# A sparse-attention and gated-MLP kernel: every convolution tap on VectorE, and a new order and new engine choices for all its jobs

## The chip, the cores and the metric

The kernel runs on one core of one Trainium2 chip. The metric is the time of one execution on the device in microseconds (us). Three runs of the kernel before gave 330.38, 330.82 and 330.89 us; the median, 330.82 us, is the time before.

## The reference

Three stages follow one another (B = 2, H = 8, S = 768, D = 64; the model width is 512). Attention sees 16 keys to either side and 24 summaries of 32 keys each; a gated layer mixes the rows with a 768 x 768 matrix; a second gated layer has a convolution of three taps along the rows.

```python
def attention(q, k, v):
    k_sum = k.reshape(B, H, 24, 32, D).max(axis=3)
    v_sum = v.reshape(B, H, 24, 32, D).mean(axis=3)
    scores = concat([where(abs(i - j) < 16, q @ k.T / sqrt(D), -1e9),
                     q @ k_sum.T / sqrt(D) + log(32)])
    a = softmax(scores)
    return a @ concat([v, v_sum])

def first_layer(x):
    u, v = split(maximum(x @ w_in, 0))
    v_n = (v - mean(v)) / sqrt(var(v) + 1e-6)
    return (u * (w_spatial @ v_n + b_spatial)) @ w_out

def second_layer(x):
    h = maximum(x @ w_in2, 0)                       # 512 -> 1024
    conv = sum(conv_w[k] * shift(h, k - 1) for k in range(3))
    return (h * sigmoid(conv)) @ w_out2             # 1024 -> 512
```

## The kernel before

All products are made at fp32 accuracy from three fp32r matmuls (`mm3`, L320 to L322: high times high, high times low, low times high). So every operand is split into a high part (a cast, L295, on ACT or POOL) and a low part (a subtraction, L289, on DVE or POOL).

**Attention** runs in 16 groups G0 to G15. A group is four head-rows of one batch; two groups share one pair of loads (n = group // 2). Each group goes through scores (PE, L472, L479, L485, into one of two PSUM tiles `s`), row maximum (DVE, L489), exponentials (ACT, L493, 12 pairs of instructions), total and reciprocal (DVE, L496, L499), the normalising multiplication (L502, POOL or DVE), two transposes (PE, L506, into the single PSUM tile `pt`) each followed by a copy out (L528, ACT or DVE), the product with the values (PE, L512) and the split of its result (L533, L534). The values of a pair of groups come by the DMA of L386 into `vwin`; there are two such buffers, used in turn, so the values of G4 (n = 2) can be loaded only when the L512 products of G0 (n = 0) are done. PE makes the block means of the values (L428), DVE and POOL the block maxima of the keys (L408, L414).

**First layer.** The weights are rounded by hand into fp32r parts (L304 to L311, the two long ones L309 and L311 on DVE). Products u and v (L550), the statistics of v, the spatial product with its operands split 768 columns wide (L600 to L602, the subtraction is L289), the gate. `w_out` is merged with the second layer's `w_in2` (L664, L665), and the merged matrix is rounded again (L689 to L699).

**Second layer.** `i2(f)` for f = 0 to 7 makes one eighth of h; `conv_gate(f)` (L736 to L790) makes its convolution: tap k = 1 is a scaling on ACT (L748), tap k = 0 a multiply-add on DVE (L752). The tap k = 2 is a second L752, except for f in `TAPDMA` = (0, 2): there ACT scales h into a tile of its own (L748, `tmp`), and two DMAs, issued on POOL's queue, add this tile to the sum (L765, one for each batch). Sigmoid (ACT, L772), gate (L775, L789). The last product uses a scheme of blocks with seven products instead of eight, with sums of blocks before (L716; some by a DMA on POOL's queue, `TDMA`, L714) and after (L874), and stores the output (L870).

**What sets the order.** `Plan.add` (L105) lists jobs, each with the engines that may run it and with what it reads and writes. `Plan.order` (L127) issues them in the order of a table `ORDER` (two letters name one job), and `PICK` says, for a job that more than one engine may run, which one. Every engine then runs its instructions in exactly that order. Where the plan sees PE idle early on, it puts warm-up matmuls with no result there (L932).

```python
if f in TAPDMA:
    add(scaled(zp, hp, 2, n), r + 0.6, [hp.tok(), tok("conv")], [zp.tok()], lock=True)
add({"DVE": (us, lambda bs=bs: tap(0, bs))}, r + 1, [hp.tok(), tok("conv")], [cp.tok()], lock=True)
if f in TAPDMA:
    for b in range(b0, b1):
        def join(b=b):
            POOL.dma_start(two(ct)[:, b, :S - 1], two(z)[:, b, 1:], accum_op=ADD)
        dma_add(r + 2, S, join, [z.tok(b * S, (b + 1) * S)], [ct.tok(b * S, (b + 1) * S)])
else:
    add({"DVE": (us, lambda bs=bs: tap(2, bs))}, r + 2, [hp.tok(), tok("conv")], [cp.tok()], lock=True)
```

Of the kernel before, what the change touches and what calls it, by code (L numbers as in the profile page):

```python
# [50 lines left out]
ORDER = (
    "ABASACAFAEAUAGAiATADAHAjAgAkAAAhALAqAVAWAIAMBKBYAXArAYA3BaAZAsANAJBbBZBLA4BcAbAtBEAKBiAuBFAaBMAOA5B8AlCRBNBjA6A7AvBGAcBO"
    "BkCTAwA8AmAxCUB9BlAyAPBHBmBvCSCDB+AnBPDJCVApBnAzA9B-AoA+CbBwBxBRA-DKA0CcCdBABoBpCoC5A1DIBIByDLCEA2BBBdBzCpBqBQBCCeDHBDB0"
    "CFAdDRBeBrBTCGCqB1CHDSAQCrBJC6CfBfCWCsC1BgB2ARC7BhDeCgB3BsDTB4ETEeDfBtBuCXEgBSChCYB5CiC2CZCjDUB6CkCBDVCACtFOEUEhB7DrEfC8"
    "CuEnCCC9BUClDWDgEoDwCaCvDhCwCmCxEpDiDjE0FPCnDXCyCzFMDMDYDxDZDsE1FBC0DaDkFCDNBVDODPCICJDlEqFVC4C+E2DbF8DmDcDnDtDyDdDQCKC-"
    "DoErFWFNEsDpAeFiEtDqBWE3AfF9C3EuE4FXFjDuDvDzEvD1D2D3F6D4CLDAD0D6CMEwFkBXD5E5EiD7DBE6FYEVCNCODCFvCPDDEXFZDEFlE7D8EjCQD9D+"
    "D-E8EYEEEkGmFFDFDGEFEAEGJ5EmE9ElEZEWF7EaEHEBEbFzECFGFDEcFHGDGQExFIFJFaEIEdFmE+EDGlEOGdFQEPGREyEJFKEKF1F0E-FLEQEzGkGSELGn"
    "EREMFAESHRGEF2F3FRGeFbENFxF4HHFcGFGTGfGgF5HIFdGhGiFSHSFwGGFnGjG6FTF+G7GtHJGUHTFeFoHKFpHUFqFfGHHLFrFUGuFgFsHVHbFhGIGvFtFu"
    "J6GwHMHlHmHcHNHdG8HnGJHOHeGKIyGVIiHfGLGMF-GAG9HoGWFEHvHWHwGXHgGBGCGYHxHpHqH5GZGaGbGNIDH6FyGoIEGxGcGyGOGPG+GzHyHXG-GpG0Gq"
    "H7HYHPGsLNItHrH8HzHhHQHiH9G1G2H+IFIIGrHAINIOHBHjHCH0HsG3HDH1HkHEIuG4H2G5IJLPHZIKHtHFIdHuH-H3IPHGILIAIaISITIeIzIvIfIjIMIG"  # L60
    "IBIbIHIgIhIUI9HaIVICJHH4InLOJIJJIkJlIoIcJ7IWI0JbIQIRIXI3IYIpI+IZI-I4JAJcI6JRIlJmImIwI5IqJKI7JSLbLQIxJdJBLUI1JTI2JnJUKHLR"
    "JLJvJCJDI8JoIrJEJeIsJVJpJwJ9JMJWJFJqJfJxKRKIJgJrLWJyJNKlJGK5KvKwKbJzLDK6LSJsKJJXLEJ0KSJOKcLTJhJiJ1JtLVKmJ+K7KKJ2LFKTLXJ3"
    "KdLYJYJ-KxJPLiLGLZJZKnLdLaKUKVJuKAKyJaLcLeJ8LfLgJQLhLkKLK8KMLpLjKoKzJ4KBLlJjLmKeKWKCKNJkKfLrK9KOKXLwLnLHMrKgKDLoLqKYLsLt"
    "LyKZKpKELIMhKqMiKhKrM1LuK+LvKFLxKsKaLzKtL0NJKPMsKGNKMjL3L1KQK0K-K1L+LJL2M2MtL5M-KuL4M3L6M4K2NLL7KiNAMAL8NdL9NMLKMkNBNnKj"
    "L-MFLAMuNCMBNTMlLBKkNDMCMvNUNoMDMHMmNVMnK3NpMELCMGK4MIMMM5NqNeNEMJMwMOOpMTMKMoMLLLNFMNMxOqM6M7MyNWNNMPMpMQO7LMNXMVMRO8MS"
    "MaNGMqM8MUMzMWNrNHOvNYOwMXNxNONsM9O9MYM+MZNtNfO1NPMbNZOrNQOxOyOzNyMcN4MdPTMeOsO+NzNuNgMfN0PBOtO2N-NhO3PHN1OuO0MgNRN6NaNi"
    "M0N5PIPJN7PKOAO4OBN8PCPUO5N9PVO-PZPDOGO6NIOIPjPEPAS9NvP0OHOUNbPaONPWNjPeOJNwPNPfNkPLPbNcOKOCNlODNSN2NmPOPcOLPkPFPgPlPXOE"
    "PmPhPPOPN3OVOWPYOOP1S+OiPMTDPdOXPnPiOYOQOZPQOMPGORP+TEPoP5ObP6OFPqP-PpP2OjOdOcPrOkP7PsP8P3OeQAOfOSPRPtQBPuOlQQQRP9OgP4QS"
    "N+PSQCQDQmQTOTPvOaOmQUPwOhQwQrQEQVQLQMQWOnQFQXTFQNQOS-QYQnQxQoQsQGQHOoQtQuPxQyQpPyQzTAQPQ9RHQZQaRCTJRDQITGTPQJQbRIRETBRF"
    "PzTLQcQKQdTCQvTHRJRKTKQ+TMTNRSQ-RAQfTITOQ0QqRcTRQeRdTWRXTVRTQ1URTQReTZQhTSUlRUTcQ2QgRGQ3QiRVQjRLTTRfTURYRZUSTdRBRaRMRnUT"  # L70
    "Q4RoRsRpRtQ5QkTgRNRqRWROQlRgRPRQQ6RuRbRvRRSASFRhQ7RrUgSBUWRiRjSCSGUmSDRxSHRwR2Q8RlUhR3RkUnUUSKSoUpUoR4S1R8UbUqUXStRmR+UY"
    "SIUiRyUZSJRzR0SESZSeUVSuSPSvUaSLUcSMUwU7SNSaSbSQUxSfR1S2UjUrSpU8R5UdUySRSwSqSOSgScSSUeSjR6SVS3SkR7ShSdVZVdSTUkU0SrSiTaSx"
    "T3UfTeSUVaR9SlSmVeSXSWSnUzU1ThVbTxSzVfU2SyT9ULR-UsVGS4U9SYS5U3TyUJUNUtU-SsU+T4U4U5VHS0VXUKTzS6VAVIT5VmVCT+U6T0UDUEVhUMWR"
    "TXVDUuT6VgVRVJVnUPS7UvVBTfWWVSUOVNVTVoVEWXT1ViVcVOT-VjVVS8UFVMT7VkVFTYWSVKUATqWTV5VlVPWbVpWYTjWlWcT2V6VqVLUQUGTlVWVrVsV-"
    "WmWAWUTsWZVyWBTmWnUBTtVzTbVtWaVuUCVQWwWxWgTiWVV0WdTkUHTnV1WpV2XdVvWhVwWeToWCWyV3VUWoTrWqXZXaV7W7TuWfTpXeWsV8W0WzW8W1WFTv"
    "WiWLTwXGWjXHWGVYWrW3WMXbWuWkWHWNXfXTWtW9WOWIWvXcWPXXWJXVXgW+XmW4W2XCXIX5XDW-X-XJW5XhXiXnXNUIW6XoXjX6XOXpV4XKWQXRV9YAXkXq"
    "XyXzXBXlXAXLX0XEXMXFXPX1WDXrXsXtX2XWXSX7XuYBWEX3YLXUXQXvYMXYX4YCXwX8YNX9WKYOV+YFT8VxX+YGYHYIYDYEYPYQYJXxYK"
)
# [999 lines left out]
```

## Time and profile before

| | |
|---|---|
| time, median of three runs | 330.82 us (330.38 to 330.89) |
| time of the profiled execution | 332.48 us |
| its span in the profile | 330.7 us |
| granted clock of TensorE | 1.00 throughout |
| busy: PE, DVE, ACT, POOL | 320.4, 270.9, 206.5, 109.3 us |

The span runs from the first instruction to the last; the profiled execution's own time lies 1.8 us above it, and 1.7 us above the median. Busy times are sums over the span. PE is TensorE's matmuls, DVE VectorE, ACT ScalarE, POOL GpSimd, SP the engine that issues most DMAs. All times below are in us unless ns is written.

### The profile page before, as it was taken

How to read it: one execution, taken by the hardware profiler on the slowest of the kernel's cores; microseconds unless marked ns; L12 is line 12 of the kernel's file. 1: busy time of each engine (PE TensorE's matmuls, PEld its weight loads, DVE VectorE, ACT ScalarE, POOL GpSimd, SP SyncE). 2: the span in 40 equal slices, each digit the busy share in tenths (PEclk: the TensorE clock that was granted, in tenths of full speed). 3: DMA queues.
4: the chain of work that ended last, by engine and by line, in shares of the span. 5: the costliest groups of instructions: out<-in, count | busy, mean ns of one | idle time of the engine just before them, and what ended most of it. 6: DMA issues, size and time to landing. Idle time of an engine off the chain costs nothing.

```text
span 330.7 us, 6432 instructions
## 1 busy us (share of the span) xinstructions
PE 320.4 (97%) x2414; PEld 272.0 (82%) x2414; DVE 270.9 (82%) x501; ACT 206.5 (62%) x516; POOL 109.3 (33%) x129
## 2 busy tenths in 40 slices
...
GB/s 236 321 210 236 238 288 157 273 135 72 2 63 51 192 140 34 107 133 66 126 92 116 152 87 127 127 97 1 96 25 22 52 68 2 43 126 119 50 113 152
DMA packets 16640, 39.25 MB, mean 119 GB/s; under 512 B 2016, under 2 KB 8160, under 8 KB 16608
## 3 DMA queue, kind: packets, MB, share of 16 engines
...
## 4 chain that ended last, share of the span: by engine, by line
PE 85%; DVE 9%; DMA 2%; ACT 2%; issue 1%; DVEq 0%
PE late L320 11%; PE late L321 11%; PE late L322 11%; PE mm L320 8%; PE mm L321 8%; PE mm L322 8%; PE xp L321 3%; PE pt L506 3%; PE pt L321 3%; PE xp L322 3%; PE pt L320 3%; PE pt L322 3%; PE xp L320 3%; PE xp L512 3%; DMA a<-vwin 2%; DVE a L311 2%
## 5 line engine op out<-in xcount | busy, mean ns | idle before, releaser
L493 ACT ACTIVATE a<-s,a 128x120 f32<-128x120 f32 x96 | 33.2, 375 | 2.1 <-DVE a L489 2.1
L289 POOL TENSOR_TENSOR w<-a,w 128x256 fp32r<-128x256 f32 (+1 forms) x14 | 14.8, 1058 | 38.5 <-ACT w L295 38.2
L322 PE MATMUL late<-xh,a 128*128 128x512 f32 (+1 forms) x72 | 26.7, 371 | 0.0
L321 PE MATMUL late<-xl,a 128*128 128x512 f32 (+1 forms) x72 | 26.7, 371 | 0.0
L320 PE MATMUL late<-xh,a 128*128 128x512 f32 (+1 forms) x72 | 26.7, 371 | 0.0
L502 POOL TENSOR_TENSOR a<-a,a 128x720 f32<-128x720 f32 x15 | 21.3, 1422 | 9.5 <-DVE a L499 7.5
L295 ACT CAST xh<-tmp 128x384 fp32r<-128x384 f32 (+2 forms) x32 | 15.8, 510 | 9.1 <-DVE tmp L716 5.6
L752 DVE SCALAR_TENSOR_TENSOR w<-v,conv_t,w 128x1534 f32<-128x1534 f32 x10 | 18.2, 1816 | 4.0 <-ACT w L748 3.8
L493 ACT ACTIVATION_READ_ACCUMULATOR a<-s,a 128x1 f32 x96 | 21.3, 222 | 0.0
L311 DVE SCALAR_TENSOR_TENSOR a<-a,a 128x512 uint32<-128x512 uint32 (+1 forms) x24 | 18.6, 776 | 0.6
L506 PE MATMUL pt<-ident,a 128*120 128x128 f32 x96 | 16.4, 280 | 2.1 <-DVE a L528 1.8
L289 DVE TENSOR_TENSOR xl<-tmp,xh 128x384 fp32r<-128x384 f32 (+2 forms) x31 | 17.9, 586 | 0.1
L528 ACT COPY a<-pt 120x384 f32<-120x384 f32 x24 | 11.6, 482 | 9.5 <-PE pt L506 9.3
L575 DVE BATCH_NORM_STATS2 stat<-tmp 128x6 f32<-128x512 f32 x12 | 8.3, 691 | 11.2 <-ACT tmp L572 11.1
L304 ACT ACTIVATE a<-a 128x512 f32<-128x512 f32 (+1 forms) x16 | 10.1, 629 | 11.4 <-POOL w L289 4.5
L309 DVE SCALAR_TENSOR_TENSOR a<-a,a 128x512 uint32<-128x512 uint32 (+1 forms) x24 | 16.0, 665 | 1.4 <-ACT a L304 0.8
L489 DVE TENSOR_REDUCE a<-s 128x6 f32<-128x720 f32 x16 | 14.2, 890 | 3.4 <-PE s L485 3.4
L295 ACT CAST w<-a 128x512 fp32r<-128x512 f32 (+1 forms) x16 | 9.1, 566 | 12.3 <-DVE a L311 12.1
L506 PEld LDWEIGHTS pt<-ident,a 128*120 128x120 f32 x96 | 10.7, 137 | 7.0 <-DVE a L528 2.5
L320 PE MATMUL mm<-xh,a 128*128 128x512 f32 (+1 forms) x44 | 16.0, 364 | 0.0
L322 PE MATMUL mm<-xh,a 128*128 128x512 f32 (+1 forms) x44 | 16.0, 364 | 0.0
L321 PE MATMUL mm<-xl,a 128*128 128x512 f32 (+1 forms) x44 | 16.0, 364 | 0.0
...
## 6 DMA issues: line engine op xcount, KB each, us to landing
...
```

The costliest lines, as they stand in the source:

```text
L289: eng.tensor_tensor(out=lo.r(), in0=src.f(), in1=hi.f(), op=ALU.subtract)
L295: us = {"ACT": (0.2 + n / 1200, lambda: ACT.copy(hi.r(), src.f())), "POOL": (0.12 + n / 1050, lambda: POOL.tensor_copy(hi.r(), src.f()))}
L309: add({"DVE": (0.16 + n / 960, lambda: DVE.scalar_tensor_tensor(out=last.u(), in0=fu.u(), scalar=0x80000000, in1=last.u(), op0=ALU.bitwise ...
L311: add({"DVE": (0.16 + n / 960, lambda: DVE.scalar_tensor_tensor(out=fu.u(), in0=fu.u(), scalar=3, in1=last.u(), op0=ALU.logical_shift_left ...
L320: PE.matmul(ps, lhsT=lh, rhs=rh, start=first and i == 0, stop=False, **kinds)
L321: PE.matmul(ps, lhsT=lh, rhs=rl, start=False, stop=False, **kinds)
L322: PE.matmul(ps, lhsT=ll, rhs=rh, start=False, stop=last and i == n - 1, **kinds)
L489: DVE.tensor_reduce(out=st[:, 0], in_=sv, op=ALU.max, axis=AX.X, negate=True)
L493: ACT.activation(out=e[:, u, :NK], in_=sv[:, u // GA, u % GA], func=AF.Exp, bias=st[:, 0, u:u + 1], accum_out=sm[:, u, :1])
L502: eng.tensor_tensor(out=e, in0=e, in1=st[:, 1].unsqueeze(2).to_broadcast([128, GB, NK]), op=ALU.mult)
L506: PE.transpose(pt3[:NK, a], e[:, GA * h + a, :NK], ident)
L752: DVE.scalar_tensor_tensor(out=two(ct)[:, bs, to], in0=two(h)[:, bs, of], scalar=scale(k), in1=two(ct)[:, bs, to], op0=ALU.mult, op1=ALU.add)
```

## The change

The tables `ORDER` and `PICK` are new, and `TAPDMA` is empty.

```diff
 ORDER = (
-    "ABASACAFAEAUAGAiATADAHAjAgAkAAAhALAqAVAWAIAMBKBYAXArAYA3BaAZAsANAJBbBZBLA4BcAbAtBEAKBiAuBFAaBMAOA5B8AlCRBNBjA6A7AvBGAcBO"
+    "AAACABADAFAgAEAiAGAjAZAaAkAhAbAHAqAcAdAeArALBYAfAMBZBbBaBcAIA3A4AsAJAlAtASAUATAVAWAuAvANBiBjAKBEA5A6A7BFCTCRCUBkAmAnAwAx"
...
 PICK = (
-    "111111010100101001011100110000000010000101001100010010000001110000001200101000110100011101110000001010100010100011000100"
+    "001101210000101011001110100010000010100011000100011010100010111010000100010001010101001100011111011000011000100000000001"
...
-TAPDMA = (0, 2)
+TAPDMA = ()
```

For f = 0 and f = 2 the tap k = 2 becomes a second L752 on DVE, in place of one L748 and two L765 each. The jobs are 1545 instead of 1553, and their order differs from the first one on. The choice of engines differs too: of the 768-wide subtractions (L289) all six now run on DVE, where before four ran on POOL and two on DVE; of the copies L528 eleven run on DVE (before eight); of the normalising L502 two run on DVE (before one). The sums of blocks that go by DMA (`TDMA`) stay. PE's products are the same; of the warm-up matmuls 22 stand in the program instead of 24.

**Place 1: PE, the transposes of the first two groups.** `s` holds scores, `pt` the transposes, `xp` the product with the values; a_0_91 and a_0_96 are the exponentials of G0 and G1. Before:

```order
96 L428 MATMUL mm_85<-a_0_233,a_0_86 24x128 x6
97 L506 MATMUL pt<-ident,a_0_91 120x128 x3
98 L428 MATMUL mm_85<-a_0_233,a_0_86 24x128 x6
99 L506 MATMUL pt<-ident,a_0_91 120x128 x3
...
116 L485 MATMUL s_81<-a_0_95,a_0_231 64x120 x12
117 L506 MATMUL pt<-ident,a_0_96 120x128 x3
...
134 L485 MATMUL s_80<-a_0_90,a_0_151 64x120 x12
135 L506 MATMUL pt<-ident,a_0_96 120x128 x3
136 L512 MATMUL xp<-a_0_92,a_0_233 64x64 x12
```

And now:

```order
89 L428 MATMUL mm_85<-a_0_236,a_0_86 24x128 x6
90 L506 MATMUL pt<-ident,a_0_91 120x128 x3
...
107 L485 MATMUL s_81<-a_0_95,a_0_252 64x120 x12
108 L506 MATMUL pt<-ident,a_0_91 120x128 x3
...
125 L485 MATMUL s_80<-a_0_90,a_0_162 64x120 x12
126 L506 MATMUL pt<-ident,a_0_96 120x128 x3
127 L512 MATMUL xp<-a_0_92,a_0_236 64x64 x12
128 L506 MATMUL pt<-ident,a_0_96 120x128 x3
```

Between the two transposes of G0 there now stand the scores of G3 in place of block means, and the first L512 (that of G0, after which the values of G4 can be loaded into `vwin`) stands ahead of the second transpose of G1 instead of behind it.

**Place 2: DVE, from the row maximum of G1 to the first copy of a transpose.** L307, L309 and L311 round weights, L499 is the reciprocal for which L502 waits, L528 the copy for which the next transpose waits. Before:

```order
28 L489 TENSOR_REDUCE a_0_95<-s_81 128x6
29 L307 TENSOR_SCALAR a_0_97<-a_0_124 128x256
30 L496 TENSOR_REDUCE a_0_90<-a_0_90 128x6
31 L499 RECIPROCAL a_0_90<-a_0_90 128x6
32 L307 TENSOR_SCALAR a_0_97<-a_0_195 128x256
33 L309 SCALAR_TENSOR_TENSOR a_0_97<-a_0_195,a_0_97 128x256
...
36 L499 RECIPROCAL a_0_95<-a_0_95 128x6
37 L309 SCALAR_TENSOR_TENSOR a_0_97<-a_0_124,a_0_97 128x256
38 L311 SCALAR_TENSOR_TENSOR a_0_195<-a_0_195,a_0_97 128x256
39 L408 TENSOR_REDUCE a_0_90<-a_0_91 128x12
40 L528 COPY a_0_92<-pt 120x384
```

And now:

```order
29 L489 TENSOR_REDUCE a_0_95<-s_81 128x6
30 L496 TENSOR_REDUCE a_0_90<-a_0_90 128x6
31 L307 TENSOR_SCALAR a_0_97<-a_0_156 128x256
32 L309 SCALAR_TENSOR_TENSOR a_0_97<-a_0_156,a_0_97 128x256
33 L311 SCALAR_TENSOR_TENSOR a_0_156<-a_0_156,a_0_97 128x256
34 L499 RECIPROCAL a_0_90<-a_0_90 128x6
35 L489 TENSOR_REDUCE a_0_90<-s_80 128x6
...
37 L499 RECIPROCAL a_0_95<-a_0_95 128x6
38 L408 TENSOR_REDUCE a_0_90<-a_0_91 128x12 x2
39 L528 COPY a_0_92<-pt 120x384
```

No L309 or L311 stands between a reciprocal L499 and the copy L528 any more: the one pair of them is ahead of the first L499.

**Place 3: DVE, the convolution of f = 0 and f = 1.** L752 is a tap, L775 the gate behind the sigmoid; w_1_2380 (now w_1_2376) is the sum of f = 0. Before:

```order
346 L752 SCALAR_TENSOR_TENSOR w_1_2380<-v_1_2362,conv_t,w_1_2380 128x2x767
...
357 L752 SCALAR_TENSOR_TENSOR w_1_2440<-v_1_2430,conv_t,w_1_2440 128x2x767 x2
358 L289 TENSOR_TENSOR a_2_2352<-a_2_2349,a_2_2352 128x256
359 L775 TENSOR_TENSOR w_1_2380<-v_1_2362,w_1_2380 128x1536
```

And now:

```order
349 L752 SCALAR_TENSOR_TENSOR w_1_2376<-v_1_2340,conv_t,w_1_2376 128x2x767 x2
...
357 L775 TENSOR_TENSOR w_1_2376<-v_1_2340,w_1_2376 128x1536
358 L697 SCALAR_TENSOR_TENSOR a_2_2320<-a_2_2320,a_1_1521 128x512
359 L752 SCALAR_TENSOR_TENSOR w_1_2448<-v_1_2436,conv_t,w_1_2448 128x2x767 x2
```

Both taps of f = 0 now stand on DVE, and its gate comes ahead of the taps of f = 1. The same second L752 is added for f = 2.

## Rows read from the trace of the kernel before

**Rows 1.** Page, part 1: busy time, share of the span and instructions of each engine.

```profile
PE 320.4 (97%) x2414; PEld 272.0 (82%) x2414; DVE 270.9 (82%) x501; ACT 206.5 (62%) x516; POOL 109.3 (33%) x129
```

**Rows 2.** Waits of PE from 0 to 110 us: total, times, longest.

```profile
PE mm L428 <- DMA a<-vwin: 1.9, 2, 1.7
PE pt L506 <- DVE a L528: 1.8, 2, 1.2
```

**Rows 3.** Waits of PE from 110 us to the end.

```profile
PE xp L321 <- DVE xl L289: 0.4, 1, 0.4
```

**Rows 4.** Timeline of PE, 8 to 28 us: start, duration, instruction, [idle before <- releaser].

```profile
8.92 1.90 PE L932 MATMUL mm<-ones 128*128 128x512 bf16 x8
...
17.12 0.54 PE L506 MATMUL pt<-ident,a 128*120 128x128 f32 x3 [1.16 <-DVE a L528]
...
20.33 0.92 PE L512 MATMUL xp<-a,a 120*64 120x64 f32 x24
...
27.92 1.49 PE L428 MATMUL mm<-a,a 96*24 96x128 f32 x12 [1.73 <-DMA a<-vwin]
```

**Rows 5.** Chain of waits, 8 to 28 us: start, duration, what.

```profile
8.80 2.17 ACT a L493 x12
...
11.66 1.54 DVE a L309
...
16.61 0.47 DVE a L528
...
21.29 6.58 DMA a<-vwin
```

**Rows 6.** Timeline of DVE around 26 us, and of POOL around 12 us.

```profile
25.91 0.42 DVE L309 SCALAR_TENSOR_TENSOR a<-a,a 128x256 uint32<-128x256 uint32 x1
...
11.53 1.39 POOL L502 TENSOR_TENSOR a<-a,a 128x720 f32<-128x720 f32 x1 [0.34 <-DVE a L499]
```

**Rows 7.** Windows: length, busy time of each engine, clock, DMA share, GB/s.

```profile
60.00:70.00 10.00, 9.86 (x141) 8.14 (x133) 9.83 (x14) 6.40 (x22) 6.59 (x6) 1.00 0.86 271
...
205.00:258.00 53.00, 53.00 (x235) 43.91 (x234) 48.62 (x60) 43.27 (x64) 7.91 (x9) 1.00 0.26 58
258.00:290.00 32.00, 32.00 (x173) 30.35 (x172) 30.13 (x49) 28.52 (x61) 6.55 (x8) 1.00 0.26 47
290.00:316.00 26.00, 25.56 (x146) 24.89 (x145) 21.68 (x43) 13.34 (x31) 13.85 (x14) 1.00 0.40 86
```

**Rows 8.** Chain of waits, at 68 us.

```profile
68.18 1.78 DVE a L311
```

**Rows 9.** Timeline of PE at 70 us.

```profile
70.47 0.54 PE L506 MATMUL pt<-ident,a 128*120 128x128 f32 x3 [0.61 <-DVE a L528]
```

**Rows 10.** Groups by line and form: busy, mean ns of one | idle before, releaser.

```profile
L752 DVE SCALAR_TENSOR_TENSOR w<-v,conv_t,w 128x1534 f32<-128x1534 f32 x10 | 18.2, 1816 | 4.0 <-ACT w L748 3.8
L765 POOL DMA_DIRECT2D w<-tmp x4 | 3.8, 1090 | 25.7 <-ACT a L295 16.2 <-ACT a L690 9.5
L289 POOL TENSOR_TENSOR a<-tmp,a 128x768 fp32r<-128x768 f32 x4 | 7.5, 1889 | 15.1 <-ACT a L295 15.1
L289 DVE TENSOR_TENSOR a<-tmp,a 128x768 fp32r<-128x768 f32 x2 | 1.9, 952 | 2.4 <-ACT a L295 2.4
```

**Rows 11.** Timeline of DVE: the first taps of f = 1, and two L716 at the end.

```profile
220.57 3.67 DVE L752 SCALAR_TENSOR_TENSOR w<-v,conv_t,w 128x1534 f32<-128x1534 f32 x2 [0.76 <-ACT w L748]
...
307.45 0.56 DVE L874 TENSOR_TENSOR w<-pt,w 128x384 f32<-128x384 f32 x1 [1.15 <-PE pt L322]
...
308.44 0.55 DVE L716 TENSOR_TENSOR a<-tmp,w 128x384 f32<-128x384 f32 x1
...
309.38 1.38 DVE L716 TENSOR_TENSOR tmp<-tmp,w 128x384 f32<-128x384 f32 x1
```

**Rows 12.** Timeline of POOL and of PE, 309 to 315 us.

```profile
309.13 1.20 POOL L716 TENSOR_TENSOR a<-a,sp 128x384 f32<-128x384 f32 x1 [1.78 <-DVE a L716]
...
313.85 0.45 PE L321 MATMUL xp<-xl,a 128*128 128x384 f32 x1 [0.44 <-DVE xl L289]
```

More of the change, by code (lines that the diff above doesn't have):

```diff
@@ L56 @@
[L56 to L75, printed above, removed]
@@ L76 @@
-    "WiWLTwXGWjXHWGVYWrW3WMXbWuWkWHWNXfXTWtW9WOWIWvXcWPXXWJXVXgW+XmW4W2XCXIX5XDW-X-XJW5XhXiXnXNUIW6XoXjX6XOXpV4XKWQXRV9YAXkXq"
-    "XyXzXBXlXAXLX0XEXMXFXPX1WDXrXsXtX2XWXSX7XuYBWEX3YLXUXQXvYMXYX4YCXwX8YNX9WKYOV+YFT8VxX+YGYHYIYDYEYPYQYJXxYK"
+    "AAACABADAFAgAEAiAGAjAZAaAkAhAbAHAqAcAdAeArALBYAfAMBZBbBaBcAIA3A4AsAJAlAtASAUATAVAWAuAvANBiBjAKBEA5A6A7BFCTCRCUBkAmAnAwAx"
+    "AOBvAyAzA8B8CVDJCSBGBwB9DKCbAoApBlBmBnAXDLA9A0A+CcA-BADHDIBxBHBoBRCoBSA1A2BBCdByBzB0BpBqCpBCAYCeAPBdCfCgBDB+DRBrB1B2C1Be"
+    "BfBgBhDSEgCqCrCsB3DwEhB-AQCDDeDfB4CEBsChBICWCtBtBuCiDTBKBLEeBJBMBTBNBOCFDgCXCYCjARB5BUCZB6BVCGCHCICJB7C2CAEnETDUDVEoDrCk"
@@ new lines @@
+    "CuClCmCnEfCKC3CvCwCaDhDMBPDWBQFNE0DiCxEpCyCzDXC0DYEqErDsCBDxDNDODPBWDjFMDZDaDAC5DtDQFOFPDkDlC6DbDcE1E2DmDnCCDyEUFVDdDoEs"
+    "EtDpEuC7C8C9C+C-BXEiDqDBCLFiEvFjE3E4EjEkDzD0EwFvCMCNDuDvCOCPD6DCDDDED7D8D9D1D+D2EEEFD3FBCQEGE5EmDFDGFkEHEIE6D4F6F7EOEPEQ"
+    "ERGmD5F8F9C4FCD-EAEBECFWEXE7FFFGEYEZEaEbGnFHFIFJFKElFXEDE8GlEcEdE9FYFLGkFZFlFaGQGRGDE+ExEJEKELESHRGSGEGFEyFmE-FAFnEzFbFz"
+    "F0EMFwGtG6GdEVJ8FQFRFcFdF1ENHHHIGeF2F3GfGGGgF4FeHSFSFTF5FoHJFUHTGhGiGjFpFqFrGuFDG7HUHVHKHLEWFsG8GTGUGHF+GVGIFtHMHNFuFfFg"
@@ new lines @@
+    "HlHmFxHnHoGJFyG9G+HOHWHbHcGvGKGwHdHXFhHpHYItGLGMF-GxGyGAHZH5GBHqIDH6HeGWGXIyGCH7FEGoH8HPHfHgGYHrHvGNGZGaGbHwHxHaGOGcGPHh"
+    "G-J5GzJ6GpG0HQH9H+HyGqLNIEG1G2GsGrH-IFIuHAHzH0HBIzINIOIPHCIIIvHsIAHiH1H2HtHuHDH3H4IBICIXIiI0HEG3IJIKHFLOLPHGILISI1G4G5Hj"
+    "I2HkITInIdIaIUIQIYIZIMLQIjIqIVIWIkIlIGIRIoIpI6LRIHIbIcI3JHJIJJImIrIeJbLbI9I+JKIwJvI7IsJ7LUI8IfIxIgI4I5KHJLJMJNKIJwI-J9JA"
+    "KbKJJBJCJDJxJcJRLWJSJTJyKcJEJUKKJdKLJFJ+JVJGJWKdJXKRKeKSJOJPKlJeIhKMKfKgJQJzJlJYJmJnJoLDJZJ-JfKvJ0JaJ1JgJhKNJ2KOJ3JpKPK5"
@@ new lines @@
+    "JiJjJ4JqK6KTJkKmLSLTLVJrJsKwLEKQKnKxKAJtLXKULYJuLZK7LiKBLaKhLcKVLdLeLFLfKCKWKyLGLgKoKzKiKpLkLHKDLhK8MhKjLjMrKXM1K9LIKkMs"
+    "KYLlLmKEM2LpMiKZKqK+LnK0MtLoKaLrKFLqM3LsLtKGM4LuLvMuKrK1LJMjMkLwLxLKNTLyNJLzL0L1MlKsMvK2MmM-L3KtNAL+K-NBNUL2L4MnLAL5L6K3"
+    "LLNCL7NVM5NdOpMwMoL8NKMpKuNnL9LBMFK4M6L-MAMBMCMHLMNeMDM7MxNDMEMGM8NfNgMyM9O1NLMIMzMMMJOqMOM+MKMLMNO2NoMqOrM0NMOvNhNNNiO3"
+    "NEMPOsNWNOMQMROwLCNpMSNFMTNjOtNPMUMVNkMaMWMXMYNQNXNYNRPNOxO7NqNGOuO4NxMZNZMbNSMcMdO5MePZNyMfNrNsNzN0O8N1OyOzO6N4PBN2NtN5"
```

20 lines of the change are left out of this document (14 added, 6 removed).

## The prediction, made before the changed kernel was run

> **What bounds the kernel now.** I read the busy times first, then the waits of the busiest engine, then the chain that ended last, and only then the prices of what the change touches. PE is busy for 320.4 of the span's 330.7 us [rows 1], so whatever moves the time must either give PE less work or take away some of the roughly 10 us in which it stands still. PE's real work is the same in both kernels, which leaves its waits. From 110 us to the end the profile finds one, of 0.4 us [rows 3]. Before 110 us there are two kinds over 1 us [rows 2]: 1.9 us on a load of the values, of which 1.73 in one piece at 27.92 us, and 1.8 us on copies of transposes, of which 1.16 at 17.12 us [rows 4]. The reader is to see that the convolution, where the change has its name from, lies in a stretch in which PE waits for nothing: from 205 to 258 us it is busy for 53.00 of 53.00 us [rows 7].
>
> The chain tells where the two early waits come from. DVE rounds weights (L309) from 11.66 us for 1.54 us, though the same form takes 0.42 us at 25.91 us [rows 5, 6]; during all of it POOL normalises (L502, 11.53 us for 1.39 us [rows 6]). Behind that, with a second stretched rounding, comes the copy L528 at 16.61 us, for which the second transpose of G0 waits until 17.12 us. So the first L512 runs at 20.33 us, the load into the buffer that it frees is on its way from 21.29 us for 6.58 us, and the block means (L428) start at 27.92 us [rows 4, 5].
>
> **The change part by part.**
>
> *Front of the program.* Places 1 and 2 show two things. No rounding stands between the reciprocals and the first copy any more, and G3's scores stand between the two transposes of G0, work that PE did later before. G0's normalising starts about 0.9 us later than before (the three roundings of 0.27 + 0.42 + 0.42 us, unstretched, stand ahead of its reciprocal; L307's 0.27 us is my estimate from its form), hence at about 12.4 us instead of 11.53 [rows 6]; it takes 1.39 us, so the first transpose comes at about 13.9 us. The copy then comes at about 15.0 us instead of 16.61 [rows 5], the second transpose at about 15.5 instead of 17.12, and the first L512 at about 17.9 instead of 20.33 [rows 4]. So the wait of 1.16 us goes (−1.16).
>
> *The load.* With the first L512 2.4 us earlier, the values for G4 land at about 21.29 + 6.58 − 2.4 = 25.5 us [rows 5]. Between this L512 and the L428 that reads them stand five transposes at about 0.5, three score groups at about 0.9, two L512 at 0.92, one small product of 0.7 and four warm-up matmuls at 0.24 (1.90 for eight [rows 4]): 8.7 us, so PE gets there at about 26.6 us, after the landing. The wait of 1.73 us goes (−1.73).
>
> *Warm-up matmuls.* Twenty-two instead of twenty-four, at 0.24 each [rows 4]: −0.48, in the same stretch, at the bound between nothing (they fill a wait that stays) and −0.48. I take −0.48 and let the next term carry the waits.
>
> *New waits.* With PE earlier, ACT is late next. It needs 2.17 us for the exponentials of one group [rows 5], and scores of a group need the `s` tile that the exponentials two groups back have emptied. I walked the first 35 us by these durations: about 0.5 us at G4's scores, 0.2 and 0.5 at the transposes of G2 and G3. Nothing of this has a row of its own. Bounds: nothing at one end, and at the other the whole of 3.4 us, if ACT, which is almost as late as PE there, sets the pace. I take +1.25, by the walk. So PE is ahead by 1.16 + 1.73 + 0.48 − 1.25 = 2.1 us at about 31 us.
>
> *From 54 to 76 us.* Here the chain runs through DVE, not PE: DVE is busy for 9.83 of the 10 us from 60 to 70 [rows 7], and PE waits 0.61 us for a copy at 70.47 us [rows 9], behind a rounding stretched to 1.78 us [rows 8]. Up to the last rounding of these weights the new order gives DVE about 1.5 us more (two copies L528 at 0.47 [rows 5], one normalising and one cast more, some small ones fewer). If DVE's idle time before that shrinks by PE's lead, as it should where DVE waits for PE's scores, it finishes 0.6 us earlier than before, against a PE that comes 2.1 us earlier and had about 0.7 us in hand at that product: 2.1 − 0.6 − 0.7 = 0.8 us of the lead is lost. Bounds: nothing lost, and 3.0 lost if the idle time does not shrink at all. I take +0.7.
>
> *Subtractions from POOL to DVE.* Four L289 of 768 columns leave POOL, 1.889 us each, and cost DVE 0.952 each [rows 10], +3.8 us of DVE. They belong to the spatial product, and PE waits for nothing from 110 us on [rows 3]. I cost them at nothing; what hides them is DVE's idle time between 76 and 205 us. Without that cover they are the first part of the rival on DVE below.
>
> *The taps.* For f = 0 and f = 2 a second L752 at 1.816 us is added, so +3.63 us on DVE; two L748 leave ACT, and four L765, 1.09 us each, leave POOL's queue [rows 10]. DVE idles 53.00 − 48.62 = 4.4 us in the stretch of the convolution and 1.9 us in the next [rows 7], and before the first taps of f = 1 it waits 0.76 us for ACT [rows 11]. From that point to the end DVE has the same work as before within 0.6 us. The tap of f = 0 lies ahead of that point, beside merges. I cost the taps at nothing, between −0.3 (sigmoid and gate of f = 0 no longer wait for a DMA) and +3.63.
>
> The rows of the profile leave the DMA way of a tap costing DVE nothing. The Trainium skill, SBUF — State Buffer, section Who interferes with whom, says more: a DMA uses ports of its own and never contends with a computing engine. By that rule the change gives up a free transfer for 3.63 us of an engine that is 82% busy, and the sum would be that of the first rival.
>
> *End.* Nothing moves by intent; the stores at the end come in the same order. 0, between −1.1 and +0.5.
>
> **The sum.** −1.16 − 1.73 − 0.48 + 1.25 + 0.7 = −1.4 us. The profiled execution took 332.48 us (span 330.7 and 1.8 around it), so 331.1 there; the median of the runs lies 1.7 lower, 330.82, so I forecast **329.4 us**. The forecast's own range is 328.4 to 330.4.
>
> **The rivals.**
>
> *DVE becomes the bound in the last third (slower).* The subtractions and the taps find no idle time in the right place, and the last products wait for their sums. For it: DVE is busy for 30.13 of 32 us from 258 to 290 us [rows 7]. Against it: it still waits 1.15 us for PE at 307.45 us [rows 11], and before the taps for ACT. Price: 3.63 − 1.15 = +2.5 on the −1.4, so 331.9 us. It decides when DVE comes to the first taps of f = 1 more than 0.8 us later, measured against PE's products, than now (220.57 us).
>
> *DVE eats the lead at 54 to 76 us (no change).* DVE's idle time doesn't shrink, or ACT holds the front back. For it: 9.83 of 10 us. Against it: part of DVE's time there is stretching, 1.78 in place of 0.7 or so, which another neighbour on POOL may not bring. Then the lead of 2.1 is lost whole: 330.8 us, and at its worst 0.9 more, 331.7.
>
> *The stretching at the end goes too (faster still).* At 309.38 us DVE's L716 takes 1.38 us against 0.55 just before, while POOL runs an L716 of its own at 309.13 us, and PE then waits 0.44 us and loses about 1.1 around it [rows 11, 12]. A new order may not bring the two together. Then 329.4 − 1.1 = 328.3, and with nothing lost at 54 to 76 us 327.6. For it: place 2 takes the roundings away from beside L502. Against it: POOL still has some ten such operations in the last 40 us. The Trainium skill, same page and section, makes this a rule: a VectorE instruction with two inputs in SBUF and a GpSimd one that reads SBUF exclude each other for a whole instruction. The stretched rows agree with it (1.54 beside L502, 0.42 alone); by the rule alone, moving four long subtractions off POOL speaks for this rival.
>
> *The change does not do what it says:* excluded, as place 3 shows the taps on DVE.
>
> **How the numbers follow.** Forecast 0.46, DVE in the last third 0.16, lead eaten 0.22, faster still 0.16. A measurement of this kernel tells 0.2%, 0.66 us, from no change. Faster by more: nearly all of the forecast (0.43), the last rival (0.16), a little of the third (0.02), together 0.61. Same: 0.03 + 0.02 + 0.13 = 0.18. Slower: 0.14 + 0.07 = 0.21. The range takes in the faster rival to 327.4 and the slower ones to 332.0.
>
> **What would show it.** Right: no wait of over 0.5 us at the first L428 on values for n = 2; the first L512 at about 18 us; L428 at 26 to 27 us; PE's waits before 110 us down from about 5 to about 3.5 us; PE without waits in the convolution. Wrong: the first L512 at 20 us or later; DVE busy without a gap from 50 to 76 us and PE waiting over 1.5 us for it there; a wait of PE on L752, L775 or L789; new waits on L289 behind 290 us.

## The result and the profile after

The changed kernel takes 325.67 us (median of four runs, 325.51 to 326.38) against 330.60 us for the kernel before: a ratio of 0.9859, 95% interval 0.9841 to 0.9876, or 4.7 us by the ratio (the medians lie 4.9 us apart). It moved the way that was forecast, but more than three times as far, and below the range. Run once more with the experiments below it gave 325.76 us, ratio 0.9898 (0.9856 to 0.9940). Of these six runs one, 330.00 us at a granted clock of 0.994, is of a slower state and does not enter that ratio, while one of 328.55 us does and pulls it up.

The page, part 1, of the changed kernel [beside rows 1]:

```profile
PE 317.9 (98%) x2412; PEld 272.3 (84%) x2412; DVE 266.5 (82%) x507; ACT 204.0 (63%) x516; POOL 101.0 (31%) x119
```

DVE was given two more long taps (3.6 us), four more long subtractions (3.8 us) and some copies, and yet it is busy for 4.4 us less. So its instructions became shorter. The groups of the two roundings show it, first in a second profile of the kernel before, then in the changed kernel (out<-in, count | busy us, mean ns of one | idle before):

```profile
L311 DVE SCALAR_TENSOR_TENSOR a<-a,a 128x512 uint32<-128x512 uint32 (+1 forms) x24 | 18.1, 755 | 0.6
L309 DVE SCALAR_TENSOR_TENSOR a<-a,a 128x512 uint32<-128x512 uint32 (+1 forms) x24 | 16.6, 690 | 1.3 <-ACT a L304 0.8
```

```profile
L311 DVE SCALAR_TENSOR_TENSOR a<-a,a 128x512 uint32<-128x512 uint32 (+1 forms) x24 | 14.5, 602 | 0.8
L309 DVE SCALAR_TENSOR_TENSOR a<-a,a 128x512 uint32<-128x512 uint32 (+1 forms) x24 | 14.4, 600 | 1.6 <-POOL a L305 0.3
```

The same 48 instructions take 34.7 us before and 28.9 after. No form changed; what changed is what POOL runs beside them. In the second profile of the kernel before seven of the 48 take 0.90 to 1.65 us, each with POOL at work beside it for 0.6 us or more. In the changed kernel every one of them takes 0.41 to 0.43 us (256 columns) or 0.68 to 0.69 us (512 columns), and POOL is at work beside them for less than 0.1 us in all. Added up over all of DVE (each instruction's time on its queue above the lower quartile of its own form in both traces), the stretching is about 29 us before and 16 after; the level depends on the quartile, the difference of 13 us hardly. Of these 13 us, 7.4 lie in the first 75 us and 2.6 behind 300 us (the kernel before by its second profile).

The waits of PE in the changed kernel, 0 to 110 us [beside rows 2]; from 110 us to the end there is none [beside rows 3]:

```profile
PE mm L932 <- DVE mhalf L926: 1.0, 1, 1.0
PE pt L506 <- DVE a L528: 0.6, 1, 0.6
PE s L485 <- DMA a<-q_in: 0.2, 1, 0.2
PE pt L506 <- POOL a L502: 0.2, 1, 0.2
PE s L472 <- issue: 0.2, 1, 0.2
```

Timeline of PE [beside rows 4]:

```profile
15.20 0.54 PE L506 MATMUL pt<-ident,a 128*120 128x128 f32 x3
...
17.17 0.92 PE L512 MATMUL xp<-a,a 120*64 120x64 f32 x24
...
24.36 0.54 PE L506 MATMUL pt<-ident,a 128*120 128x128 f32 x3 [0.61 <-DVE a L528]
...
27.79 2.80 PE L428 MATMUL mm<-a,a 96*24 96x128 f32 x24
```

The second transpose of G0 starts at 15.20 us (17.12 before), the first L512 at 17.17 (20.33), and the block means at 27.79 us wait for no load. The windows [beside rows 7] show PE without a gap in the convolution and at the end, though DVE is busier in the convolution, 50.38 us instead of 48.62:

```profile
60.00:70.00 10.00, 10.00 (x126) 8.22 (x122) 8.48 (x17) 8.98 (x32) 4.27 (x4) 1.00 0.69 193
...
205.00:258.00 53.00, 53.00 (x237) 44.04 (x236) 50.38 (x58) 42.50 (x71) 8.59 (x7) 1.00 0.11 19
290.00:316.00 26.00, 26.00 (x152) 26.00 (x151) 20.11 (x45) 10.27 (x23) 12.33 (x13) 1.00 0.33 85
```

At the end, no L716 on DVE lasts 1.38 us any more, as it did beside POOL's L716 [rows 11, 12]; timelines of DVE and POOL after:

```profile
305.58 0.55 DVE L716 TENSOR_TENSOR tmp<-tmp,w 128x384 f32<-128x384 f32 x1
306.05 0.55 DVE L289 TENSOR_TENSOR xl<-a,xh 128x384 fp32r<-128x384 f32 x1
...
308.90 0.56 DVE L874 TENSOR_TENSOR w<-mm,v 128x384 f32<-128x384 f32 x1 [1.16 <-PE mm L322]
```

```profile
303.11 1.01 POOL L289 TENSOR_TENSOR xl<-tmp,xh 128x384 fp32r<-128x384 f32 x1 [0.58 <-ACT xh L295]
307.17 1.44 POOL L289 TENSOR_TENSOR xl<-tmp,xh 128x384 fp32r<-128x384 f32 x1 [3.06 <-ACT xh L295]
```

POOL still subtracts there, but at 303 and 307 us, and DVE's seven operations from 304.18 to 307.74 us lie in between, but for the last: there it is POOL's subtraction that lasts longer, 1.44 us in place of 1.01.

### The profile page after: what moved, and what is told of

It reads as the page before. It is cut to its first block, busy times and chain, and to the rows that moved or that the text cites. A ratio compares the mean times of both kernels' runs of the same rounds, so it can differ in the third digit from the quotient of the medians.

```text
span 324.1 us, 6397 instructions
## 1 busy us (share of the span) xinstructions
PE 317.9 (98%) x2412; PEld 272.3 (84%) x2412; DVE 266.5 (82%) x507; ACT 204.0 (63%) x516; POOL 101.0 (31%) x119
## 4 chain that ended last, share of the span: by engine, by line
PE 93%; ACT 2%; POOL 2%; DMA 1%; DVE 1%; issue 1%; SPq 0%; POOLq 0%
PE late L321 11%; PE late L320 11%; PE late L322 11%; PE mm L320 10%; PE mm L321 10%; PE mm L322 10%; PE pt L506 3%; PE pt L321 3%; PE pt L320 3%; PE pt L322 3%; PE xp L321 3%; PE xp L320 3%; PE xp L322 3%; PE xp L512 3%; PE s L485 2%; DMA a<-q_in 1%
## 5 line engine op out<-in xcount | busy, mean ns | idle before, releaser
L289 POOL TENSOR_TENSOR w<-a,w 128x512 fp32r<-128x512 f32 (+1 forms) x15 | 15.5, 1039 | 37.4 <-ACT w L295 37.2
L752 DVE SCALAR_TENSOR_TENSOR w<-v,conv_t,w 128x1534 f32<-128x1534 f32 x12 | 22.1, 1845 | 2.8 <-ACT w L748 2.6
L580 POOL TENSOR_TENSOR stat<-stat,mhalf 128x1 f32<-128x1 f32 x12 | 7.9, 660 | 45.6 <-DVE stat L577 41.9
L502 POOL TENSOR_TENSOR a<-a,a 128x720 f32<-128x720 f32 x14 | 19.7, 1414 | 6.0 <-DVE a L499 3.1
L289 DVE TENSOR_TENSOR a<-tmp,a 128x256 fp32r<-128x256 f32 (+2 forms) x27 | 15.8, 597 | 6.8 <-ACT a L295 6.8
L714 POOL DMA_DIRECT2D tmp<-w x9 | 8.1, 968 | 41.0 <-ACT tmp L713 34.0
L295 ACT CAST a<-tmp 128x256 fp32r<-128x256 f32 (+2 forms) x28 | 14.8, 540 | 8.5 <-DVE tmp L581 6.3
L304 ACT ACTIVATE a<-a 128x512 f32<-128x512 f32 (+1 forms) x20 | 12.5, 624 | 8.6 <-POOL w L289 4.9
L506 PE MATMUL pt<-ident,a 128*120 128x128 f32 x96 | 16.5, 281 | 1.0 <-DVE a L528 0.6
L289 DVE TENSOR_TENSOR xl<-tmp,xh 128x384 fp32r<-128x384 f32 (+2 forms) x29 | 15.7, 551 | 0.7 <-ACT xh L295 0.5
L309 DVE SCALAR_TENSOR_TENSOR a<-a,a 128x512 uint32<-128x512 uint32 (+1 forms) x24 | 14.4, 600 | 1.6 <-POOL a L305 0.3
L506 PEld LDWEIGHTS pt<-ident,a 128*120 128x120 f32 x96 | 10.8, 136 | 5.5 <-POOL a L502 1.2
```

The source lines that it names most:

```text
L289: eng.tensor_tensor(out=lo.r(), in0=src.f(), in1=hi.f(), op=ALU.subtract)
L295: us = {"ACT": (0.2 + n / 1200, lambda: ACT.copy(hi.r(), src.f())), "POOL": (0.12 + n / 1050, lambda: POOL.tensor_copy(hi.r(), src.f()))}
L304: mul = {"ACT": (0.2 + n / 1080, lambda: ACT.mul(fu.f(), half(1).bitcast(F32), 2.0 ** -112)), "POOL": (0.18 + n / 1050, lambda: POOL.tenso ...
L309: add({"DVE": (0.16 + n / 960, lambda: DVE.scalar_tensor_tensor(out=last.u(), in0=fu.u(), scalar=0x80000000, in1=last.u(), op0=ALU.bitwise ...
L502: eng.tensor_tensor(out=e, in0=e, in1=st[:, 1].unsqueeze(2).to_broadcast([128, GB, NK]), op=ALU.mult)
L506: PE.transpose(pt3[:NK, a], e[:, GA * h + a, :NK], ident)
```

## The experiments

My theory after the result: the gain is DVE time that was stretched beside POOL and lay ahead of a wait of PE, in the first 76 us and at the end (stretched: longer than the same form takes elsewhere); the taps are hidden. Rivals: the taps by DMA cost the time; the subtractions moved off POOL did it; the gain is PE's new order alone. Each run stands beside runs of the kernel before on the same chip (330.47 to 330.62 us in median), and ratios are against those.

**The kernel before, profiled again.** No edit.

> The kernel before, unchanged, profiled once more. It tells which of its losses belong to the program and which to the one execution profiled (its own time was 332.48 us, 1.7 above the median). Every theory expects 330.6 us within 0.7. If the stretched roundings beside POOL belong to the order, the second transpose of G0 starts at about 17 us again, the first block means on reloaded values wait 1.5 us or more again, and the copy at 70 us and the three stretched operations at 309 to 313 us come again. If they were chance, some are missing.

It gave 330.40 us, ratio 1.0002 (0.9985 to 1.0018); its profiled execution took 330.22 us, span 328.4. Its waits of PE, 0 to 110 us:

```profile
PE pt L506 <- DVE a L528: 1.4, 2, 1.1
PE mm L932 <- DVE mhalf L926: 1.0, 1, 1.0
PE s L485 <- DMA a<-q_in: 0.4, 1, 0.4
PE xp L512 <- DVE xl L534: 0.3, 1, 0.3
PE pt L506 <- POOL a L414: 0.3, 1, 0.3
PE xp L512 <- DVE a L447: 0.3, 1, 0.3
PE s L472 <- ACT a L493: 0.2, 1, 0.2
```

The wait for the copy is there again, so are the stretched roundings at 11 and 14 us and the three stretched operations at the end. The wait of 1.73 us for the load [rows 4] is not: it belonged to the one execution profiled first, which was 1.7 us slower than the median. Against this second profile the changed kernel's PE is ahead as follows. I matched the two by the work that PE still has to do, every job at its usual duration, and took the second profile of the changed kernel (span 323.4). Up to 60 us the jobs come in different orders, so there the figures are good to some tenths of a us:

| PE's work still to do | where | PE is ahead by |
|---|---|---|
| about 290 us | at 29 us | about 1.5 us |
| about 260 us | at 62 us | 2.5 us |
| about 250 us | at 70 us | 3.5 us |
| 15 us | at 304 us | 3.8 us |
| 10 us | at 309 us | 4.7 us |
| end of the span | | 5.1 us |

**Taps on DVE in the old order.**

```diff
-TAPDMA = (0, 2)   # and 5 jobs for each of the two
+TAPDMA = ()       # one L752 right behind the first
```

> The order and the engines of the kernel before, with only the taps k = 2 of f = 0 and 2 turned into a second L752 right behind the first. My theory (the gain is DVE time that was stretched beside POOL, in the first 76 us and at the end, and the taps are hidden): 330.6 us within 0.9. Rival (the taps by DMA cost the time: four DMA issues on POOL's queue, the DMAs and two scalings on ACT): most of the 4.7 us gain, so 326 to 327.5 us. The rival that the taps on DVE cost: 332 us or more.

330.83 us, ratio 1.0014 (0.9999 to 1.0029). The taps by themselves change nothing that can be told from noise: the interval runs from no change to 1.0 us more, so most of the 3.63 us more on DVE is hidden.

**One tap by DMA again in the new order,** first with its scaling in ACT's queue, then on POOL.

```diff
-TAPDMA = ()
+TAPDMA = (0,)
```

> The changed kernel with the tap k = 2 of f = 0 put back to a scaling on ACT and two adding DMAs, all else in its order. My theory: 325.7 us within 0.7. Rival (taps by DMA cost the time): 327 to 329 us, half of the gain or more lost, since one of the two is back.

> The changed kernel with the tap k = 2 of f = 0 by DMA again, its scaling on POOL instead of in ACT's queue. My theory (with the scaling on ACT, PE waited 1.8 us for a relu behind it, and the DMAs themselves cost nothing): 325.7 us within 0.7, and no wait of PE for L732. Rival (a tap by DMA costs time in this order in any way): 327 us or more.

329.10 us, ratio 0.9962 (0.9936 to 0.9988), and 331.72 us, ratio 1.0025 (1.0006 to 1.0043): both miss my theory, and in this order the tap by DMA costs time, as the rivals had it. ACT's timeline, f = 0's scaling and sigmoid, with the scaling on ACT, then on POOL, then in the changed kernel's second profile:

```profile
204.45 1.56 ACT L748 ACTIVATE tmp<-v,conv_t 128x1536 f32<-128x1536 f32 x1
...
213.65 1.28 ACT L772 ACT_TABLE_LOAD   x1 [4.95 <-DMA w<-tmp]
```

```profile
216.44 1.28 ACT L772 ACT_TABLE_LOAD   x1 [7.68 <-DMA w<-tmp]
```

```profile
208.44 1.28 ACT L772 ACT_TABLE_LOAD   x1 [1.44 <-DVE w L752]
```

The new order puts the sigmoid of f = 0 into ACT's queue close behind the taps. With the tap on DVE it starts at 208.44 us; with the DMA it stands there until the sum has landed, and the relus of f = 1 (L732) queue behind it. PE waits for them, 1.8 us in the first run and 3.7 in the second (waits of PE from 110 us to the end, one kernel each):

```profile
PE mm L320 <- ACT v L732: 1.8, 1, 1.8
```

```profile
PE mm L320 <- ACT v L732: 3.7, 1, 3.7
```

The medians lie further above the changed kernel's than these waits, by 3.4 and 6.0 us. In the second run part of the rest is PE's clock: right behind the wait of 3.7 us its granted clock was 0.50, the lower of its two levels (1.2 GHz), from 220 to 222 us, and 0.71 from 222 to 224 us, where the changed kernel has 1.00. I estimate 1.6 us of work lost from these two shares. In the first run the profiled execution took 327.81 us with the clock at 1.00 behind the wait; four of its ten executions had a mean clock of 0.993 to 0.995 and took 330.3 to 333.1 us. The window of the second run (length, busy PE, PEld, DVE, ACT, POOL, clock, DMA share, GB/s):

```profile
220.00:222.00 2.00, 2.00 (x5) 1.61 (x6) 1.71 (x2) 1.97 (x3) 0.00 (x0) 0.50 0.00 0
```

In the old order the sigmoid stood behind those relus (218.31 us in the second profile of before, when the DMA issued at 212.06 had landed) and waited for nothing. So the taps on DVE gain nothing by themselves, but this order would lose 3 us and more without them. The cause that I expected, ACT's scaling, was wrong: with it off ACT the wait was longer, not shorter. (On POOL the scaling put the DMAs later as well, at 208.58 us in place of 207.02.)

**Orders cut and joined.** The first 481 jobs of the new order, or the first 280 (to about 50 us), followed by the others in the old one.

```diff
-order = old
+order = new[:481] + [job for job in old if job not in new[:481]]     # or 280
```

> The first 481 jobs in the changed kernel's order and with its engines, all the others in the order and with the engines of the kernel before, taps by DMA as there. My theory: the lead of PE is 5 us at 76 us as in the changed kernel and the stretched operations at the end (1.0 us) come back: 325.7 + 1.0 = 326.7 us within 0.9. Rival (the gain comes from the later part, the subtractions on DVE and the taps): 329 to 331 us.

> The first 280 jobs (to about 50 us) in the changed kernel's order and with its engines, the rest as before. At 50 us PE should be ahead by about 1.4 us. My theory (from 50 to 76 us the old order, with 4 to 5 us of stretching on DVE, is bound by DVE, so that a lead is lost there): the lead at 76 us is 0.6 us or less, 330.1 us or more. Rival (PE is the bound there but for single waits, and a lead stays): the lead at 76 us is 1.2 us or more, 329.3 us or less.

329.27 us, ratio 0.9966 (0.9939 to 0.9993), and 334.30 us, ratio 1.0118 (1.0102 to 1.0135). In the first, PE is ahead of the second profile of before by 3.5 us at 70 us, as in the changed kernel; then it loses 1.7 us at the joint, where PE waits for an ACT operation that the old order puts late, and the wait of 0.4 us at the end is back. Its time lies in the rival's range (329 to 331 us), not in mine (326.7 within 0.9). The wait at the joint:

```profile
PE mm L320 <- ACT tmp L572: 1.3, 1, 1.3
```

In the second PE loses over 5 us at the joint: it waits 2.4 us for a relu L595 and 1.4 us for L502, and behind these waits its granted clock was 0.50 from 56 to 58 us. So the front does hold the lead, but a time for it cannot be read from such joints, and the question put to the run with 280 jobs was not answered.

**Single pieces in the old order.** (a) The first copy of G0 ahead of a rounding; (b) two places between 60 and 70 us; (c) POOL's three operations at the end on DVE; (d) all three; (e) place (b) without its mistake; (f) a, c and e together.

```diff
 # (a) DVE
+L528 COPY            first transpose of G0
 L311 SCALAR_TENSOR_TENSOR
 L408 TENSOR_REDUCE
-L528 COPY
 # (b) and (e) DVE, 60 to 70 us
-L311 SCALAR_TENSOR_TENSOR
 L435 TENSOR_REDUCE
+L311 SCALAR_TENSOR_TENSOR
...
-L307 TENSOR_SCALAR
 L534 TENSOR_TENSOR   x2
 L489 TENSOR_REDUCE
+L307 TENSOR_SCALAR
 L309 SCALAR_TENSOR_TENSOR
+L528 COPY            first transpose of G10; (b) only
 L311 SCALAR_TENSOR_TENSOR
-L528 COPY            (b) only
 # (c) engine of one L716 and two L289, 309 to 313 us
-POOL
+DVE
```

> The kernel before with one step moved on DVE: the first copy of G0's transpose (L528) runs ahead of the stretched rounding L311 instead of behind it and a block maximum. Warm-up matmuls as before. My theory: the second transpose of G0 starts at about 16.0 instead of 17.1 us and nothing later takes that back: -1.1 us, 329.5 us. Rival (ACT's exponentials set the pace of the front, so a lead there is given back by 50 us): 330.6 us within 0.3.

329.34 us, ratio 0.9956 (0.9941 to 0.9971): −1.1 us as expected. The transpose's wait of 1.12 us is gone. The roundings are still stretched here, 1.54 and 1.14 us; what helped is that the copy no longer stands behind the second. The profiled execution took 330.79 us, 1.4 us above the median, and loses the lead again by 70 us, so only the start is read from it. Its timeline of PE:

```profile
15.39 0.54 PE L506 MATMUL pt<-ident,a 128*120 128x128 f32 x3
```

> The kernel before with the three operations that POOL runs from 309 to 313 us (one L716 and two L289) on DVE instead, at the same place of the order. DVE gets 3 x 0.47 = 1.4 us more and is no longer stretched there (2.5 us). My theory: PE's wait of 0.44 us and the 1 us lost around it go: -1.0 us, 329.6 us. Rival (the wait is DVE's work as such): 330.6 us or up to 0.4 more.

329.51 us, ratio 0.9965 (0.9947 to 0.9983): −1.0 us as expected. DVE does more and is done earlier, because nothing there is stretched: with POOL's three operations on DVE, DVE's own go from 1.37 to 0.55 us, which shows what stretched them. PE waits for nothing behind 110 us. Its timeline of DVE [beside rows 11]:

```profile
307.74 0.56 DVE L716 TENSOR_TENSOR tmp<-tmp,w 128x384 f32<-128x384 f32 x1
308.20 0.55 DVE L289 TENSOR_TENSOR xl<-a,xh 128x384 fp32r<-128x384 f32 x1
308.67 0.56 DVE L716 TENSOR_TENSOR tmp<-tmp,w 128x384 f32<-128x384 f32 x1
```

> The kernel before with DVE's order changed in two places between 60 and 70 us, so that no rounding L311 lies beside a subtraction or a normalising on POOL, and the copy of G10's transpose comes ahead of the last of them. My theory: the wait for that copy at 69 to 70 us (0.6 us and what goes with it) goes: -0.9 us, 329.7 us. Rival (DVE is the bound there by its own work, not by the stretching): 330.6 us within 0.3, the copy earlier, but the last rounded weights late in its place.

330.93 us, ratio 1.0013 (0.9988 to 1.0038): no gain. Most of the stretching went (an L309 at 1.18 us stayed), but my edit put a wait in its place, since the copy now stood ahead of a rounding and had to wait for PE's transpose; the rounding, and the exponentials behind it on ACT, came late, and PE waited 0.6 us for those:

```profile
66.83 0.56 DVE L528 COPY a<-pt 120x384 f32<-120x384 f32 x1 [1.14 <-PE pt L506]
```

> The three changes together on the kernel before. My theory: -1.1 - 0.9 - 1.0 = -3.0 us, 327.6 us, two thirds of the way to the changed kernel (325.7 us) with taps by DMA, the subtractions on POOL and nearly the old order. Rival (the new order's gain is spread over many small waits): not below 329.5 us.

329.06 us, ratio 0.9965 (0.9935 to 0.9994): 1.4 us of the 3.0 expected, with the mistake of (b) in it.

> The kernel before with two roundings on DVE moved between 60 and 65 us (an L311 behind the block means of n = 5, an L307 behind the row maximum of G12), so that both miss POOL's subtractions; unlike in the run with two places changed, the copy of G10's transpose stays behind its L311, so DVE does not wait for PE there. My theory (stretching there is on the path): DVE reaches that copy 1 us or more earlier and the wait of PE for it goes: -0.6 to -0.9 us, 329.8 us. Rival (DVE's own work and ACT's exponentials bound PE there): 330.6 us within 0.3.

330.16 us, ratio 0.9992 (0.9982 to 1.0003): 0.3 us, not told apart from no change. In its profile PE is ahead by 0.5 us at that place, less than the 0.6 to 0.9 expected. The timeline of DVE shows why: the rounding L307 is short now, and the next L311 is stretched beside L502 instead.

```profile
63.89 0.42 DVE L307 TENSOR_SCALAR a<-a 128x512 uint32<-128x512 uint32 x1
64.41 0.95 DVE L309 SCALAR_TENSOR_TENSOR a<-a,a 128x512 uint32<-128x512 uint32 x1
65.40 1.76 DVE L311 SCALAR_TENSOR_TENSOR a<-a,a 128x512 uint32<-128x512 uint32 x1
```

> The kernel before with the copy of G0's transpose ahead of its rounding, the two roundings of 60 to 65 us moved, and POOL's three operations at the end on DVE; taps by DMA, subtractions on POOL, PE's order and warm-up matmuls as before. My theory (each piece of stretching that lies ahead of a wait of PE counts by itself): -1.1 - 0.3 - 1.0 = -2.4 us, 328.1 us, half of the gain. Rival (what one piece gains is lost at the next wait): 329.0 us or more.

328.07 us, ratio 0.9924 (0.9912 to 0.9936): −2.5 us, near the sum of the pieces (−1.1 − 0.3 − 1.0). Matched as above, PE's lead in its profile is 0.9 us from 20 to 60 us, 1.7 at 70 and 2.6 at the end, so each piece lies where it was put. Three small moves on DVE and POOL are worth half of the gain, with the old order on PE, the taps by DMA and the 768-wide subtractions on POOL.

**Two pieces taken from the new order.** The four 768-wide subtractions back on POOL; the nine warm-up matmuls behind the start left out.

```diff
 # engine of four L289, 768 columns
-DVE
+POOL
 # and, in the other kernel, warm-up matmuls ahead of G0, G1 and the first transpose of G2
-6, 5, 4
+6, 0, 0
```

> The changed kernel with the four 768-wide subtractions (L289) back on POOL, all else as in it. My theory: they lie where PE waits for nothing, so 325.7 us within 0.6. Rival (POOL's long subtractions stretch DVE on the path): 326.5 us or more.

327.53 us, ratio 0.9910 (0.9896 to 0.9925): by the medians 1.8 us of the gain are lost, against the theory. PE then waits 1.0 us at 118 us, where the kernel before had no such wait. The chain to it runs from a subtraction on POOL at 106.81 us (2.01 us) through the load of the next weights that it lets go (5.61 us), their cast and the next subtraction on POOL to ACT's L572:

```profile
115.38 1.83 POOL L289 TENSOR_TENSOR a<-tmp,a 128x768 fp32r<-128x768 f32 x1 [4.77 <-ACT a L295]
117.24 0.60 ACT L572 ACTIVATE tmp<-mm 128x512 f32<-128x512 f32 x1 [1.94 <-POOL a L289]
117.89 0.39 PE L320 MATMUL mm<-a,v 128*128 128x256 f32 x1 [0.97 <-ACT tmp L572]
```

So the new order needs the subtractions on DVE. In the old order PE waits for neither taps nor subtractions, which speaks for no gain from them there; for the taps this was run, for the subtractions it was not.

> The changed kernel without the nine warm-up matmuls that stand before the scores of G1 (five) and before the first transpose of G2 (four); the thirteen at the start stay. My theory: they lie in waits of PE (for the scores' operands and for POOL's normalising), so the work behind them starts at the same time but for a few tenths: 325.7 us, between -0.6 and +0.3. Rival (they hold PE back by up to 2.1 us): 324.5 us or less. Rival (PE's clock falls without them): the granted clock under 0.95 in the first 30 us and 326.5 us or more.

326.28 us, ratio 0.9881 (0.9867 to 0.9896): no gain. The nine are worth about 2 us of PE, and PE waits instead, 1.5 us for L502 and 1.4 us for q_in; the granted clock stays at 1.00 in the first 30 us. No version that was run beats the changed kernel.

## Why the prediction was wrong, point by point

Four terms of the sum failed: the load (−1.73, which was not in the median), the new waits (+1.25, of which 0.3 is new), 54 to 76 us (+0.7, where PE gained 1.0 instead) and the end (0, which was −1.0). One stretch, 31 to 62 us, was not in the sum. In the order of the prediction:

- **The wait for the copy, −1.16: right.** The second transpose came at 15.20 us (forecast 15.5), the first L512 at 17.17 (17.9), and the step alone measured −1.1 us.
- **The wait for the load, −1.73: failed as a term.** It did go, but it was not in the median: the second profile of before hasn't got it. I had noted that the profiled execution lay 1.7 us above the median and still took a wait of just this size off the median.
- **Warm-up matmuls, −0.48: no term.** Leaving out nine more gained nothing; they lie in waits. That the two left out here gain nothing either is inferred from that, not shown.
- **New waits, +1.25: right by themselves, but set against nothing, so failed as a term.** The profile names 0.6, 0.2, 0.2 and 0.2 us, 1.2 together, all before 31 us. But the kernel before has 0.9 of its own there besides the copy's 1.1 (0.4 for q_in, 0.3 for L414 and 0.2 for the exponentials in the list of its second profile), so the net is 0.3. The sum up to 31 us was forecast as 2.1 and was about 1.5 us at 29 us: that the two lie near is luck, as the load is too large by 1.7 us and this term by 0.9 the other way.
- **31 to 62 us: not in the forecast.** PE's lead grows from about 1.5 to 2.5 us, where waits of 0.2 to 0.3 us before L506 and L512 are gone. This was read from the traces and not tested by itself.
- **54 to 76 us, +0.7: the step that failed with the wrong sign.** I counted 1.5 us more work for DVE and let it finish too late. The rows at hand said otherwise: an L311 at 1.78 us [rows 8]. The work grew, and its time shrank. In the changed kernel DVE is busy for 8.48 of the 10 us from 60 to 70 instead of 9.83, and PE's lead grows by 1.0 us instead of falling by 0.7. In the old order one repaired place gave 0.3 us by the times, and 0.5 and 0.8 us in the profiles of the two runs that had it; the rest is argued from the same stretching, not shown.
- **The end, 0: failed.** It gave −1.0 us, and the run with the three operations on DVE shows the cause. I had it as a rival, with 0.16. That POOL still has such operations there I took as evidence against. It has nine subtractions and sums of blocks in its last 40 us (eight before), and yet DVE is hardly stretched behind 300 us: it is when they run that counts.
- **Taps and subtractions at nothing: right for the taps in the old order,** where they alone measured 1.0014 (0.9999 to 1.0029); for the subtractions there it was not run. What I did not see is that the new order uses both: the sigmoid follows its taps at once, and with the subtractions back on POOL PE waits 1.0 us. That a tap by DMA takes no time of DVE did not make it the cheaper way: its sum lands late.
- **PE's roughly 10 us of standing still: not the whole budget.** The waits of PE shrink by a little over 2 us from one second profile to the other, but the span by 5.1. PE's busy time shrinks too, from 319.7 to 317.2 us with the same products and two warm-up matmuls less, so part of what a late neighbour costs is counted as busy (see the end of this text).
- **The rivals.** DVE as the bound in the last third did not come; PE is busy for 53.00 of 53.00 us. Nor was the lead eaten. The third, the stretching that goes, is the case that came, and further than priced (328.3, at best 327.6 us). The Trainium skill, SBUF — State Buffer, section Who interferes with whom, has the rule that the prediction named: a VectorE instruction with two inputs in SBUF and a GpSimd one that reads SBUF exclude each other. These runs agree: L309, L311 and L716 take 1.38 to 1.78 us beside POOL in the rows shown, and 0.42 to 0.69 alone.

The pieces of the 4.7 us, then: about 1.1 (copy), 1.0 (end) and 0.3 (one place at 60 to 65 us) are shown in the old order by themselves and add up there to 2.5. The other half is spread over the first 76 us and the last 0.4 us, the stores behind PE's last product, where only the traces speak; that PE's new order has a share of its own in it was not tested.
